# Attention feeding a mixture of experts: eight more key tiles multiplied with the values in float32

## The chip, the core and the metric

The kernel runs on 1 core of one Trainium2 chip. The metric is the device time of one execution in microseconds (us); of several executions the median is given.

## The reference

What is computed, cut to what matters (4 batches, 8 heads, 1152 keys, 576 pooled queries, head size 64):

```python
q_pool = q.reshape(B, H, S // 2, 2, D).mean(axis=3)
scores = np.matmul(q_pool, k.transpose(0, 1, 3, 2)) / np.sqrt(D)
scores = scores - np.max(scores, axis=-1, keepdims=True)
attn = np.exp(scores)
attn = attn / (np.sum(attn, axis=-1, keepdims=True) + 1e-09)
x = np.matmul(attn, v)                # all heads side by side: 2304 tokens x 512
...
h = np.maximum(x[b, s] @ w1[e], 0.0)  # e: this token's expert, by a gate on x
out[b, s] = p[e] * (h @ w2[e])
```

The change touches the product of `attn` and `v` alone.

## The kernel before, in words

The program is one order of instructions written out by hand: every engine takes its instructions in the order in which the Python code issues them, and waits where an operand isn't there. First comes the attention, then a gate that sorts tokens by expert, then the experts' two products over blocks of 128 tokens.

The attention (`attention`, L41) goes through 288 steps: 16 pairs of heads, two heads in a pair, 9 key tiles of 128 keys for each head, so 18 steps to a pair. In what follows 3:1 is step 1 of pair 3; steps 0 to 8 are the pair's first head, 9 to 17 its second. The loop at L395 issues in each step, in this order:

- `scores(s)` (L260): four TensorE matmuls of 288 columns (L268, L270) put the scores of a key tile into a PSUM tile `sc`, of which there are two, and ScalarE writes their exponentials in float32 into `ph` (L272).
- `feed_max` (L334): units of work for a later head: a matmul into a PSUM tile `psm` (L234, L240, L242; two tiles) and a VectorE maximum over it (L235, L244). The matmul that comes two units later waits for that maximum, since it needs the tile.
- preparing a later pair: GpSimd and ScalarE split keys, queries and values into two float16 parts (L155 to L203).
- in even steps `low(g)` (L278) for the two steps before. It subtracts the upper 16 bits of `ph`, read as bfloat16, from `ph` and writes the rest as float16 into `pl` (L284): a 128x576 subtraction, on GpSimd for steps 0, 2, 4, 6, 7, 10 to 14 and 16 of a pair (`LOWG`, L32), on VectorE for 1, 3, 5, 9 and 15. The other two steps, 8 and 17, have none.
- `av(s - 6)` (L296): the product of the exponentials of six steps ago with the values, added up in a PSUM tile `av`. The key tile of step 2:16 is so multiplied in step 3:4.

`av` has two forms. With float16 parts each of five query tiles takes three matmuls: upper part by the values' upper part (L310), upper by lower (L311), low part `pl` by upper (L312). In float32 (`in_f32`, L99) each query tile takes one matmul of `ph` itself by a float32 copy of the values, `vx` (L308); there `low` has nothing to do. Float32 is used for the ninth key tile of every head, and for step 13 (key tile 4 of the second head) of the nine pairs in `F32K1` (L26). `load_x` (L93) fetches the float32 values by DMA from SyncE's queue in step 8 of the pair before.

Between these steps lie smaller pieces: weights of the experts split into two parts (L586 on ScalarE, L592 on VectorE; `WSTEPS` at L463 says in which steps), the scaling of a finished head (L1302 to L1314), and for each batch of eight heads the gate's operations, one to a step, in steps of a pair that `GPL` and `GPL2` (L464, L465) allow; `GPL2` is for the third batch. Some of these use one of the two `sc` tiles under the name `wide`, as L702, L740 and L745 do, and the next `scores` but one then waits until a VectorE operation such as L741 has read it.

Of the kernel before, what the change touches and what calls it, by code (L numbers as in the profile page):

```python
# [8 lines left out]
F32 = mybir.dt.float32  # L9
# [9 lines left out]
B, H, S, D = 4, 8, 1152, 64  # L19
Q = S // 2  # L20
NKT = S // 128
# [1 line left out]
LAG = 6  # L23
LEAD = 4
SHD = 3
F32K1 = (1, 4, 5, 6, 8, 9, 12, 13, 14)  # L26
PREP0 = 13
WLEAD = 12
PRE0 = "qhb vha vl0a vl1a pqs0b pqs1b qlb loadb pkl0b pkl1b pql0b pql1b nop nop nop nop nop vhb vl0b vl1b"
# [11 lines left out]
def attention(tc, psum, stg, kT, qeo, vL, ident, emit_x, extra, load_ident, drain):  # L41
    nc = tc.nc
    V, A, G, T, SP = nc.vector, nc.scalar, nc.gpsimd, nc.tensor, nc.sync
# [5 lines left out]
    lat = late.enter_context(tc.tile_pool(name="a_late", bufs=1, side="right"))  # L49
# [6 lines left out]
    QA = [pers.tile([128, 2, Q], F16, name=f"qa{i}") for i in range(3)]  # L56

    VT = [lat.tile([128, 2, NKT - 1, 130], F16, name=f"vt{i}") for i in range(3)]
    VX = [lat.tile([128, 3, 65], F32, name=f"vx{i}") for i in range(2)]
    QD = [pers.tile([128, 128], F16, name=f"qd{i}") for i in range(3)]  # L60
    MN = [pers.tile([128, 5, 65 - 64 * i], F16, name=f"mn{i}") for i in range(2)]
    NPH = 5
    PHI = [lat.tile([128, 2 * Q + 64], F32, name=f"ph{i}") for i in range(NPH)]
# [29 lines left out]
    def load_x(p):  # L93
        b, h = divmod(2 * p, H)
        SP.dma_start(out=VX[p % 2][:, 0:2, 0:64], in_=vL[b, h:h + 2, :, 8 * D:9 * D].rearrange("h p d -> p h d"))
        if p in F32K1:
            SP.dma_start(out=VX[p % 2][:, 2, 0:64], in_=vL[b, h + 1, :, 4 * D:5 * D])

    def in_f32(n, kt):  # L99
        return kt == 8 or (kt == 4 and n % 2 == 1 and n // 2 in F32K1)  # L100

    def warm(x=None):
        x = KD[0] if x is None else x
# [171 lines left out]
    def top(x):  # L275
        return x.bitcast(BF16).rearrange("p (q two) -> p q two", two=2)[:, :, 1]

    def low(g):  # L278
        for r in range(2):
            n, kt = divmod(2 * g + r, NKT)  # L280
            if not in_f32(n, kt):
                x = G if (2 * g + r) % 18 in LOWG else V
                pf = PHI[g % NPH][:, r * Q:r * Q + Q]
                x.tensor_tensor(out=PLO[g % NPH][:, r * Q:r * Q + Q], in0=pf, in1=top(pf), op=ALU.subtract)  # L284
# [11 lines left out]
    def av(s):  # L296
        n, kt = divmod(s, NKT)
        p, j = divmod(n, 2)
        if kt == 0:
            AV[n] = ps_a.tile([128, 512], F32, name="av", tag="av")  # L300
        a = AV[n]
        ph, pl = top(PHI[s // 2 % NPH]), PLO[s // 2 % NPH]
        v = VT[p % 3]
        for t in range(5):
            o = a[:, t * 65:t * 65 + 65]
            c = (s % 2) * Q + t * 128
            if in_f32(n, kt):
                T.matmul(o, PHI[s // 2 % NPH][:, c:c + 128], VX[p % 2][:, j if kt == 8 else 2], start=False, stop=(kt == NKT - 1 and t == 4), skip_group_check=True)  # L308
                continue
            T.matmul(o, ph[:, c:c + 128], v[:, j, kt, 0:65], start=(kt == 0 and t == 0), stop=False, skip_group_check=True)  # L310
            T.matmul(o[:, 0:64], ph[:, c:c + 128], v[:, j, kt, 65:129], start=False, stop=False, skip_group_check=True)  # L311
            T.matmul(o, pl[:, c:c + 128], v[:, j, kt, 0:65], start=False, stop=(kt == NKT - 1 and t == 4), skip_group_check=True)  # L312
        if kt == NKT - 1:
            x = emit_x(n, AV.pop(n), ps_m, wide)
            later.extend(x[0])
            slow.extend(x[1])
            fast.extend(x[2])
# [46 lines left out]
    for m in MN:  # L364
        V.memset(m, 0.0)
    for x in VX:
        V.memset(x[:, :, 64:65], 1.0)
# [16 lines left out]
    f1["pkd0"]()  # L384
    f1["pkd1"]()
    load_x(0)
    f1["kl"]()
    f1["add"]()
# [6 lines left out]
    for s in range(NS + LAG):  # L395
        if s < NS:
            if not prep and nld[0] < min(NBH // 2, npr[0] + 1):
                load(nld[0])
                nld[0] += 1
            if s % 18 == 8 and s // 18 + 1 < NBH // 2:  # L400
                load_x(s // 18 + 1)
            if s % 18 == PREP0:
                p = s // 18 + 2
                if p < NBH // 2:
                    prep += prep_ops(p)
                    npr[0] += 1
            feed_shift(s)
            scores(s)
            feed_max(s)
            for _ in range(2 if s < PREP0 else 1):  # L410
                if prep:
                    prep.pop(0)()
            if s > 0 and s % 2 == 0:
                low(s // 2 - 1)
        elif s == NS:
            low(NS // 2 - 1)
        if s >= LAG:
            av(s - LAG)
# [43 lines left out]
WCD = (3, 4, 5)  # L462
WSTEPS = [30, 37, 45, 50, 54, 72, 86, 90, 125, 158, 176, 194, 230, 234, 278, 283]  # L463
GPL = {0, 1, 3, 7, 9, 13, 14, 15, 17}  # L464
GPL2 = {0, 1, 2, 5, 7, 9, 10, 11, 12, 13, 14, 15, 16, 17}  # L465
GPL1 = {9}
DMAC = {5: 0, 7: 1, 9: 0, 11: 1, 13: 0, 15: 1, 17: 0, 19: 1}
NA = 14
# [809 lines left out]
def build(tc, io, out):  # L1278
    nc = tc.nc
    V, A, G, T, SP = nc.vector, nc.scalar, nc.gpsimd, nc.tensor, nc.sync  # L1280
    with ExitStack() as ctx, tc.manual_schedule():
# [73 lines left out]
        def drain(k, wide, bank):  # L1355
# [3 lines left out]
            else:  # L1359
                first(f"d{k}")  # L1360

        tail = attention(tc, c2, m.stg, io["kT"], io["qeo"], io["vL"], m.ident2, emit_x, extra, m.load_consts, drain)
        m.open_h(c3)
        n = len(tail) - len(gate[B - 1][2])
# [28 lines left out]
```

## Time and profile before

| what | value |
|---|---|
| median of three executions | 671.71 us (670.96 to 673.86) |
| the profiled execution, its own time | 675.04 us |
| its span, from the first to the last instruction | 672.9 us |
| mean granted TensorE clock in it | 0.984 |
| TensorE matmuls busy | 642.0 us |
| VectorE busy | 552.1 us |
| ScalarE busy | 428.1 us |
| GpSimd busy | 421.4 us |
| `scores` and the products of pairs 1 to 15 | 39.80 to 417.50 us of the span |

The profile is one execution; its own time is 3.3 us over the median. A matmul's duration in it runs from its start to the end of its last column, while the next one has long begun: five matmuls of 190 ns may start 30 ns apart. So matmuls are read here by the distance between the starts of neighbours, and a step by the distance between its first `scores` matmul (L268) and the next step's. An engine's idle time says nothing by itself: what counts is the engine whose queue is never empty.

### The profile page before, as it was taken

The page shows a single profiled execution, that of the slowest core. Times are in us where ns is not written, and L with a number is a line of the kernel's source. Part 1 is how long each engine was busy: PE and PEld are TensorE (multiplying, and loading weights), DVE is VectorE, ACT ScalarE, POOL GpSimd, SP SyncE. Part 2 cuts the span into 40 slices and gives each one's busy share as a digit, 9 for nine tenths or more (in the row PEclk, how much of TensorE's full clock was granted, in tenths as well). Part 3 has the DMA queues.
Part 4 walks back from the last instruction along what each step waited for, and adds up shares of the span by engine and source line. Part 5 has one row for each costly group of instructions (what it writes and reads, how often), then busy time and mean ns, then how long its engine had stood idle before and what let it go on. Part 6 is the DMA issues. An engine that isn't in the chain of part 4 may idle for free.

```text
span 672.9 us, 22880 instructions
## 1 busy us (share of the span) xinstructions
PE 642.0 (95%) x9247; PEld 499.0 (74%) x9247; DVE 552.1 (82%) x1045; ACT 428.1 (64%) x846; POOL 421.4 (63%) x383
## 2 busy tenths in 40 slices
PE   7999999999999999999999998789999999999994
PEld 2587888888888888878887787679559649848941
DVE  7788897897998888898888897759559899899852
ACT  3678778777778677778677565559776535544500
POOL 8899999998898998898998758166000000000064
PEclk9899999999999999999999999789999999999998
DMA  8864654667474578473684307678669769777763
GB/s 245 198 173 148 201 152 111 188 163 161 140 220 113 164 180 160 139 241 90 200 181 126 108 2 133 222 236 255 208 232 325 260 237 304 287 266 260 268 235 121
DMA packets 83228, 128.80 MB, mean 191 GB/s; under 512 B 35759, under 2 KB 42031, under 8 KB 83120
## 3 DMA queue, kind: packets, MB, share of 16 engines
q1 hardware_dynamic: 79920, 117.24, 58.7%
q0 software_dynamic: 3200, 10.05, 4.3%
q8 instruction: 76, 1.25, 0.7%
q14 instruction: 32, 0.26, 0.1%
HBM read 68.82 MB, written 10.04 MB: 117 GB/s over the span
## 4 chain that ended last, share of the span: by engine, by line
PE 51%; issue 29%; DVE 10%; POOL 4%; ACT 2%; DMA 2%; another core or an unknown queue 0%; SPq 0%; POOLq 0%; DVEq 0%; ACTq 0%
PE sc L268 9%; PE sc L270 8%; PE psm L242 7%; PE av L308 6%; PE av L311 5%; PE av L310 5%; PE av L312 4%; DVE mx L244 4%; POOL out L1220 3%; DVE pl L284 2%; PE psh L257 1%; PE psh L1205 1%; PE psm L240 1%; DMA xT<-xr 1%; DVE w L592 1%
## 5 line engine op out<-in xcount | busy, mean ns | idle before, releaser
L272 ACT ACTIVATE ph<-sc 128x576 f32<-128x576 f32 x288 | 186.9, 652 | 91.8 <-PE sc L270 72.9
L244 DVE TENSOR_REDUCE mx<-psm 128x1 f32<-128x512 f32 (+1 forms) x300 | 194.1, 663 | 44.4 <-PE psm L242 41.0
L284 POOL TENSOR_TENSOR pl<-ph 128x576 f16<-128x576 f32 x167 | 207.1, 1256 | 9.0 <-ACT ph L272 9.0
L312 PE MATMUL av<-vt,pl 128*128 128x65 f16 x1235 | 138.2, 192 | 1.1 <-issue 1.1
L311 PE MATMUL av<-vt,ph 128*128 128x64 f16 x1235 | 139.1, 195 | 0.0
L310 PE MATMUL av<-vt,ph 128*128 128x65 f16 x1235 | 138.6, 193 | 0.0
L311 PEld LDWEIGHTS <-ph 128*128 128x128 bf16 x1235 | 115.3, 97 | 20.6 <-issue 0.3
L1220 POOL DMA_INDIRECT out<-acc,sid x14 | 13.7, 979 | 177.6 <-DVE acc L1129 175.4
L310 PEld LDWEIGHTS <-ph 128*128 128x128 bf16 x1235 | 116.4, 97 | 10.9 <-issue 2.9
L268 PE MATMUL sc<-qs,ks 128*128 128x288 f16 x576 | 118.0, 286 | 2.8 <-DVE st L718 1.0
L270 PE MATMUL sc<-qa,ks 65*128 65x288 f16 (+1 forms) x576 | 118.1, 286 | 0.6 <-ACT qa L258 0.6
L312 PEld LDWEIGHTS <-pl 128*128 128x128 f16 x1235 | 115.7, 99 | 1.3 <-issue 1.3
L1216 PE MATMUL pso<-w,hq 128*128 x480 | 107.4, 380 | 0.0
L592 DVE SCALAR_TENSOR_TENSOR w<-wf,w 128x512 f16<-128x512 f32 x124 | 94.3, 765 | 13.1 <-ACT w L586 12.8
L1205 PEld LDWEIGHTS <-wc 128*128 128x128 f16 x1728 | 89.2, 99 | 7.2 <-issue 6.6
L1216 PEld LDWEIGHTS <-hq 128*128 128x128 f16 (+1 forms) x576 | 45.8, 102 | 59.8 <-issue 11.7
L586 ACT ACTIVATE w<-wf 128x512 f16<-128x512 f32 x124 | 76.4, 626 | 18.0 <-DMA wf<-wq 17.8
L1205 PE MATMUL psh<-xr,wc 128*128 128x128 f16 (+1 forms) x1584 | 85.0, 212 | 1.5 <-ACT xr L1034 0.7
L242 PE MATMUL psm<-ks,qs 128*128 128x512 f16 x232 | 83.2, 379 | 0.6 <-DVE mx L244 0.6
L284 DVE TENSOR_TENSOR pl<-ph 128x576 f16<-128x576 f32 x80 | 82.4, 1030 | 1.2 <-issue 1.2
L270 PEld LDWEIGHTS <-ks 65*128 65x128 f16 (+1 forms) x576 | 56.5, 98 | 15.4 <-issue 0.8
L1071 ACT ACTIVATE hq<-psh 128x256 f16<-128x256 f32 x74 | 28.4, 384 | 52.4 <-PE psh L1205 51.6
(241 smaller groups left out, 1014.5 us busy)
## 6 DMA issues: line engine op xcount, KB each, us to landing
wf<-wq SPq DMA_DIRECT2D x124, 256.0 KB
wd<-w SPq DMA_DIRECT2D x40, 512.0 KB
ks<-kd SPq DMA_DIRECT2D x32, 288.0 KB
vf<-vL SPq DMA_DIRECT2D x16, 576.0 KB
qf<-qeo SPq DMA_DIRECT2D x15, 576.0 KB
kf<-kT SPq DMA_DIRECT2D x14, 576.0 KB
qs<-qh SPq DMA_DIRECT2D x60, 72.0 KB
ks<-kl SPq DMA_DIRECT2D x30, 144.0 KB
```

The source lines that it names most:

```text
L242: T.matmul(m[:, 0:w], q[:, t * 128:t * 128 + 128], k[:, c * 512:c * 512 + w], start=True, stop=True)
L244: V.tensor_reduce(out=mx[:, i, c:c + 1], in_=m[:, 0:w], op=ALU.max, axis=AX.X)
L268: T.matmul(sc[:, c, 0:288], ksl, QS[p][:, j, c * 288:(c + 1) * 288], start=True, stop=False)
L270: T.matmul(sc[:, c, 0:288], kal, QA[p % 3][u, j, c * 288:(c + 1) * 288], start=False, stop=True)
L272: A.activation(out=PHI[g % NPH][:, r * Q:(r + 1) * Q].rearrange("p (c q) -> p c q", c=2), in_=sc[:, :, 0:288], func=AF.Exp, scale=1.0 / 16)
L284: x.tensor_tensor(out=PLO[g % NPH][:, r * Q:r * Q + Q], in0=pf, in1=top(pf), op=ALU.subtract)
L310: T.matmul(o, ph[:, c:c + 128], v[:, j, kt, 0:65], start=(kt == 0 and t == 0), stop=False, skip_group_check=True)
L311: T.matmul(o[:, 0:64], ph[:, c:c + 128], v[:, j, kt, 65:129], start=False, stop=False, skip_group_check=True)
L312: T.matmul(o, pl[:, c:c + 128], v[:, j, kt, 0:65], start=False, stop=(kt == NKT - 1 and t == 4), skip_group_check=True)
L592: self.nc.vector.scalar_tensor_tensor(out=lo, in0=t, scalar=float(2 ** (W2S if ph % 2 else W1S)), in1=hi, op0=ALU.mult, op1=ALU.subtract)
L1205: self.nc.tensor.matmul(p[:, ft, c], u[:, ws, kk, ft * 128:ft * 128 + 128], x[:, 2 * kk + xs_, c], start=(n == 0 and ft == 0 and i == 0), ...
L1216: self.nc.tensor.matmul(p[c], h(hs, ft)[:, c], u(ws, ft), start=(first and n == 0), stop=(last and n == e), skip_group_check=(m < 128))
```

## The change

Two kinds of float32 key tiles stay as they were: the ninth of every head, and step 13 of eight of the nine pairs. A table `F32X` names further steps for each pair. Against before, 1:14, 2:16, 3:1, 3:10, 6:16, 8:1, 9:12, 12:16 and 13:15 are new, and 12:13 goes back to float16 parts: eight steps more. `vx` grows from three to five places, and `load_x` issues one DMA of 128 rows of 256 bytes for each entry. One number of `GPL2` moves, from 7 to 4.

```diff
-F32K1 = (1, 4, 5, 6, 8, 9, 12, 13, 14)
+F32X = ((), (13, 14), (16,), (1, 10), (13,), (13,), (13, 16), (), (1, 13), (12, 13), (), (), (16,), (13, 15), (13,), ())
+NVX = 3
...
-    VX = [lat.tile([128, 3, 65], F32, name=f"vx{i}") for i in range(2)]
+    VX = [lat.tile([128, 2 + NVX, 65], F32, name=f"vx{i}") for i in range(2)]
...
-        if p in F32K1:
-            SP.dma_start(out=VX[p % 2][:, 2, 0:64], in_=vL[b, h + 1, :, 4 * D:5 * D])
+        for i, x in enumerate(F32X[p]):
+            j, kt = divmod(x, NKT)
+            SP.dma_start(out=VX[p % 2][:, 2 + i, 0:64], in_=vL[b, h + j, :, kt * D:kt * D + D])
 
     def in_f32(n, kt):
-        return kt == 8 or (kt == 4 and n % 2 == 1 and n // 2 in F32K1)
+        x = n % 2 * NKT + kt
+        return n % 2 + 1 if kt == NKT - 1 else 3 + F32X[n // 2].index(x) if x in F32X[n // 2] else 0
...
-                T.matmul(o, PHI[s // 2 % NPH][:, c:c + 128], VX[p % 2][:, j if kt == 8 else 2], start=False, stop=(kt == NKT - 1 and t == 4), skip_group_check=True)
+                T.matmul(o, PHI[s // 2 % NPH][:, c:c + 128], VX[p % 2][:, in_f32(n, kt) - 1], start=False, stop=(kt == NKT - 1 and t == 4), skip_group_check=True)
...
-GPL2 = {0, 1, 2, 5, 7, 9, 10, 11, 12, 13, 14, 15, 16, 17}
+GPL2 = {0, 1, 2, 4, 5, 9, 10, 11, 12, 13, 14, 15, 16, 17}
```

Three places of the program show how it moves. In the changed kernel the lines behind the table stand one to three numbers later.

TensorE in step 3:4, the product with the key tile of 2:16 (`ph` the exponentials, `vt` the values' float16 parts, `vx` the float32 values). Before, the first of five query tiles, and the start of the next step:

```order
L234 MATMUL psm<-ks_132,qs 128x128
L310 LDWEIGHTS ph_147
L310 MATMUL av<-vt_138,ph_147 128x65
L311 LDWEIGHTS ph_147
L311 MATMUL av<-vt_138,ph_147 128x64
L312 LDWEIGHTS pl_152
L312 MATMUL av<-vt_138,pl_152 128x65
```

and now:

```order
L237 MATMUL psm<-ks_132,qs 128x128
L311 MATMUL av<-vx_139,ph_147 128x65 x5
L271 LDWEIGHTS ks_132
L271 MATMUL sc<-qs,ks_132 128x288
```

Fifteen weight loads with their matmuls became five matmuls in float32 at the same place.

VectorE from step 3:0 to step 3:6 (`mx` the maxima, `mn` their last reduction, `w` the experts' weights). Before:

```order
L592 SCALAR_TENSOR_TENSOR w_79<-wf,w_79 128x512
L244 TENSOR_REDUCE mx<-psm 128x1 x2
L284 TENSOR_TENSOR pl_153<-ph_148 128x576
L244 TENSOR_REDUCE mx<-psm 128x1
L235 TENSOR_REDUCE mx<-psm 128x4
L248 TENSOR_REDUCE mn_145<-mx 128x5
L284 TENSOR_TENSOR pl_154<-ph_149 128x576
```

and now:

```order
L595 SCALAR_TENSOR_TENSOR w_79<-wf,w_79 128x512
L247 TENSOR_REDUCE mx<-psm 128x1 x3
L238 TENSOR_REDUCE mx<-psm 128x4
L251 TENSOR_REDUCE mn_145<-mx 128x5
L287 TENSOR_TENSOR pl_154<-ph_149 128x576
```

The low part of 3:1 is gone from between two maxima; the rest of the queue moves up.

GpSimd from the end of pair 2 into pair 3 (`kl` and `ql` the lower parts of keys and queries of pair 4, `vt` its values). Before:

```order
L182 TENSOR_TENSOR kl<-kf,kd 128x576
L188 TENSOR_TENSOR ql<-qf,qh 128x576
L284 TENSOR_TENSOR pl_152<-ph_147 128x576
L203 TENSOR_TENSOR vt_137<-vf,vt_137 128x2x4x64
L284 TENSOR_TENSOR pl_153<-ph_148 128x576
```

and now:

```order
L185 TENSOR_TENSOR kl<-kf,kd 128x576
L191 TENSOR_TENSOR ql<-qf,qh 128x576
L206 TENSOR_TENSOR vt_137<-vf,vt_137 128x2x4x64
L287 TENSOR_TENSOR pl_153<-ph_148 128x576
```

The low part of 2:16 is gone from between `ql` and the values' lower part.

## Rows read from the trace of the kernel before

**Rows 1.** The page: busy time by engine (span, share), and the chain that ended last.

```profile
PE 642.0 (95%) x9247; PEld 499.0 (74%) x9247; DVE 552.1 (82%) x1045; ACT 428.1 (64%) x846; POOL 421.4 (63%) x383
...
PE 51%; issue 29%; DVE 10%; POOL 4%; ACT 2%; DMA 2%; another core or an unknown queue 0%; SPq 0%; POOLq 0%; DVEq 0%; ACTq 0%
```

**Rows 2.** Busy time by stretch: pairs 2, 3, 4, 7, 8, 10, 12, 13, 14.

```profile
core 0: us, PE busy (x) PEld busy (x) DVE busy (x) ACT busy (x) POOL busy (x), PEclk, DMA share, GB/s
66.35:90.45 24.10, 24.10 (x370) 20.24 (x367) 20.87 (x36) 19.32 (x40) 22.45 (x18) 1.00 0.56 167
90.45:114.99 24.54, 24.14 (x375) 19.63 (x372) 20.61 (x34) 18.45 (x38) 24.23 (x21) 1.00 0.50 144
114.99:139.06 24.07, 23.89 (x376) 19.64 (x372) 21.27 (x35) 18.91 (x39) 23.76 (x19) 1.00 0.60 168
...
190.17:214.41 24.24, 24.24 (x371) 20.37 (x371) 21.44 (x45) 17.57 (x36) 20.65 (x18) 1.00 0.60 181
214.41:238.23 23.82, 23.64 (x376) 19.53 (x372) 21.01 (x38) 18.50 (x38) 23.41 (x19) 1.00 0.58 159
...
264.35:290.88 26.53, 25.67 (x385) 21.14 (x382) 24.59 (x48) 20.35 (x43) 22.95 (x19) 1.00 0.50 137
...
315.00:338.83 23.83, 23.64 (x375) 19.53 (x372) 21.01 (x38) 18.51 (x39) 23.41 (x19) 1.00 0.72 174
338.83:365.23 26.40, 25.85 (x415) 21.64 (x412) 24.05 (x46) 19.71 (x42) 24.33 (x21) 1.00 0.61 162
365.23:391.93 26.70, 25.51 (x381) 21.03 (x381) 22.62 (x49) 16.82 (x35) 18.65 (x16) 1.00 0.31 95
```

**Rows 3.** Timeline of TensorE: the product in steps 1:1 (float16) and 2:1 (float32).

```profile
start us, us, engine line op out<-in xcount [idle before <-releaser]
44.02 0.19 PE L310 MATMUL av<-vt,ph 128*128 128x65 f16 x1
...
44.48 0.28 PE L268 MATMUL sc<-qs,ks 128*128 128x288 f16 x1
...
68.24 1.22 PE L308 MATMUL av<-vx,ph 128*128 128x65 f32 x10
69.30 0.29 PE L268 MATMUL sc<-qs,ks 128*128 128x288 f16 x1
```

**Rows 4.** Groups by line, shapes apart: busy us, mean ns; idle before, releaser.

```profile
L284 POOL TENSOR_TENSOR pl<-ph 128x576 f16<-128x576 f32 x167 | 207.1, 1256 | 9.0 <-ACT ph L272 9.0
...
L284 DVE TENSOR_TENSOR pl<-ph 128x576 f16<-128x576 f32 x80 | 82.4, 1030 | 1.2 <-issue 1.2
```

**Rows 5.** Timeline of pair 3, steps 3:3 to 3:7.

```profile
94.56 1.24 ACT L272 ACTIVATE ph<-sc 128x576 f32<-128x576 f32 x2
94.73 1.15 POOL L284 TENSOR_TENSOR pl<-ph 128x576 f16<-128x576 f32 x1
94.75 1.74 DVE L284 TENSOR_TENSOR pl<-ph 128x576 f16<-128x576 f32 x1
...
96.48 0.41 PE L268 MATMUL sc<-qs,ks 128*128 128x288 f16 x2
...
97.74 0.38 PE L240 MATMUL psm<-kd,qd 128*128 128x512 f16 x1 [0.22 <-DVE mx L235]
...
99.02 0.41 PE L268 MATMUL sc<-qs,ks 128*128 128x288 f16 x2
...
100.82 0.42 PE L268 MATMUL sc<-qs,ks 128*128 128x288 f16 x2
```

**Rows 6.** The same of pair 7, steps 7:5 to 7:7, where nothing waits.

```profile
196.78 0.41 PE L268 MATMUL sc<-qs,ks 128*128 128x288 f16 x2
...
198.76 0.41 PE L268 MATMUL sc<-qs,ks 128*128 128x288 f16 x2
...
200.24 0.30 PE L268 MATMUL sc<-qs,ks 128*128 128x288 f16 x1
```

**Rows 7.** The same of pair 10, step 10:5.

```profile
270.81 0.41 PE L268 MATMUL sc<-qs,ks 128*128 128x288 f16 x2
...
272.99 0.29 PE L268 MATMUL sc<-qs,ks 128*128 128x288 f16 x1
```

**Rows 8.** The same of pair 14, steps 14:3 and 14:4.

```profile
370.41 0.42 PE L268 MATMUL sc<-qs,ks 128*128 128x288 f16 x2
...
372.37 0.18 DVE L741 TENSOR_TENSOR oh<-wide,c 128x40 f16<-128x40 f32 x1
...
372.60 0.41 PE L268 MATMUL sc<-qs,ks 128*128 128x288 f16 x2 [0.85 <-DVE oh L741]
```

**Rows 9.** Waits of SyncE's queue: us in total, times, longest; then one line's DMAs.

```profile
SPq L135 <- ACT ph L272: 62.1, 10, 10.9
...
L97 SPq DMA_DIRECT2D vx<-vL x9: 457/469/1387, 27.0 to 351.1; - x9
```

**Rows 10.** Busy time in all of pairs 1 to 15: the sum over their stretches.

```profile
sum 377.70, PE 371.13 PEld 309.72 DVE 326.74 ACT 280.78 POOL 340.37; mean PE 24.74 PEld 20.65 DVE 21.78 ACT 18.72 POOL 22.69
```

## The prediction

> **What bounds the kernel now.** First the page: TensorE is busy 95% of the span and holds 51% of the chain that ended last; VectorE has 10% of it, GpSimd 4% [rows 1]. That is a mean over stages, and "busy" counts overlapping matmuls, so the next view is the busy time by pair of heads. In pairs 2 and 7 TensorE is busy for the whole stretch, 24.10 of 24.10 us and 24.24 of 24.24 [rows 2]; over pairs 1 to 15 it is idle for 377.70 - 371.13 = 6.6 us in all [rows 10]. GpSimd comes second, with 20.65 to 24.23 us busy in these stretches. The granted clock is 1.00 in all of them, the upper of the two levels (2.4 GHz), so the clock has nothing to give back here.
>
> What the reader should see in the stretches is that pairs with an extra float32 tile are not the shorter ones when nothing waits. Pair 2 holds one (1:13, multiplied in 2:1) and takes 24.10; pairs 8 and 12 hold none and take 23.82 and 23.83; pair 3 holds none and takes 24.54 [rows 2]. So there are two things to price: the float32 product itself, and the waits in pairs without it.
>
> **The float32 product.** A float16 product starts at 44.02 and the next step's scores at 44.48: 0.46 us for fifteen matmuls. A float32 one starts at 68.24 and the next scores at 69.30: 1.06 us, recorded as ten matmuls [rows 3]. Each tile that changes form costs TensorE 1.06 - 0.46 = 0.60 us. Eight more of them (nine new, one taken back) are **4.8 us** on the engine that is never empty.
>
> A page bears on this, the Trainium skill, "FP8 and Floating Point Precision", section TensorE Precision Notes: a true float32 product takes four passes through the array. With a pass as long as one float16 matmul of the trace (0.46 / 15 = 0.031 us) five query tiles would be an estimated 20 x 0.031 = 0.61 us instead of 1.06. The row differs, and I take the row; the page's case is the last rival.
>
> **What is removed.** Eight low parts: five on GpSimd (1:14, 2:16, 3:10, 6:16, 9:12; that of 12:16 goes and that of 12:13 comes back), at 1.26 us each, and three on VectorE (3:1, 8:1, 13:15), at 1.03 us [rows 4]. That is 6.3 and 3.1 us off engines with idle time. It shortens the kernel only where TensorE waits behind them.
>
> How much it waits follows from the stretches. Pair 2 without its one extra tile would take 24.10 - 0.60 = 23.50 us with no wait. Against that, pair 3 loses 24.54 - 23.50 = 1.04 us, pair 4 loses 24.07 - 23.50 = 0.57, pair 8 loses 0.32, pair 12 loses 0.33 [rows 2]. In pair 3 one sees who does it. VectorE's low part of 3:1 starts at 94.75, just behind one of GpSimd's at 94.73, and takes 1.74 us instead of 1.03; the maxima behind it are late, and the matmul of a max unit waits for L235 [rows 5]. Step 3:5 takes 99.02 - 96.48 = 2.54 us and step 3:6 takes 1.80, against 1.98 and 1.48 in pair 7 [rows 5, 6]: 0.56 + 0.32 = 0.88 of the 1.04 us. The other 0.16 stays: scores behind ScalarE's exponentials (two in a row from 94.56), which don't move.
>
> **The sum, place by place** (a tile is multiplied six steps after its scores):
>
> - 1:14, in 2:2. Pair 2 has no idle time to soak it up: **+0.60**.
> - 2:16 in 3:4 and 3:1 in 3:7. +1.20. The 0.6 us in 3:4 come just before the waits of 3:5 and 3:6, and the low part of 3:1 is gone from the queue that caused them: -0.88. **+0.32**.
> - 3:10 in 3:16. +0.60. GpSimd is one subtraction earlier when pair 4 begins, and TensorE later: most of pair 4's 0.57 should go; I take -0.45, since the same wait on ScalarE as in pair 3 (0.16) may stay. **+0.15**.
> - 6:16, in 7:4. Pair 7 is busy throughout: **+0.60**.
> - 8:1, in 8:7. Its low part is VectorE's, ahead of the max units of 8:5: -0.32. **+0.28**.
> - 9:12, in 10:0. Step 10:5 takes 272.99 - 270.81 = 2.18 us against 1.98 [rows 6, 7]; with TensorE later that 0.20 goes: **+0.40**.
> - 12:13 back to float16, 12:16 to float32: the 0.60 us move from 13:1 to 13:4; one low part for another on GpSimd. **0**, between -0.2 and +0.3, as steps 13:2 and 13:3 lose cover for up to 0.3 us of wait of the kind seen in pair 12.
> - 13:15, in 14:3. The next scores wait there: 372.60 - 370.41 = 2.19 us for a step whose work is about 1.2 (pair 7's 7:6 with its extra unit takes 1.48), because L741 on VectorE reads the `wide` tile only at 372.37 [rows 8]. L741 doesn't depend on the product, so its 0.60 us fit into that wait: **0**.
> - The number of `GPL2` moves one gate operation from 14:7 to 14:5, the gate's other operations of that lap stay; TensorE's matmuls in it are the same. **0**, 0.2 either way.
> - Eight more DMAs on SyncE, at 0.47 us each (1.39 at most) to issue, stand ahead of the key copies of L135; those wait 62 us in ten waits for ScalarE anyway [rows 9], so the cover is 6 us a time. If it failed, a pair would lose up to 1.4 us. **0**.
>
> Together 0.60 + 0.32 + 0.15 + 0.60 + 0.28 + 0.40 = **+2.35 us**. Behind the attention nothing changes; experts and gathers start that much later. The profiled execution would take 675.04 + 2.35 = 677.4; it lies 3.3 us above the median, outside the three values shown, so I add the difference to the median: 671.71 + 2.35 = **674.1 us**, 0.35% slower. A measurement of this kernel can tell about 0.5%, 3.4 us, from no change.
>
> **Bounds.** If no wait is relieved (13:15's cover aside) the cost is 4.8 - 0.6 = 4.2 us: 675.9. If all idle time of TensorE in pairs 3, 4, 8, 10, 13 and 14 is soaked up (0.40 + 0.18 + 0.18 + 0.86 + 0.55 + 1.19 = 3.36 [rows 2], and the 1.04 + 0.57 + 0.32 of waits in place of the first three's 0.76: 4.5 us), the cost is 0.3: 672.0. Values between stand nearer the forecast, since over half of that idle time (2.6 us, in pairs 10, 13 and 14) belongs to gate operations whose chain is untouched.
>
> **Rivals.**
> - *Slower: the waits stay.* What TensorE waits for in pairs 3, 4, 8 and 10 are maxima on VectorE, and a queue that is free of one low part may only wait elsewhere: VectorE also carries the weights' split at 3:0 and 4:0 and runs beside GpSimd's other subtractions, which stretch its own to 1.74 us [rows 5]. Then all that is left is the float32 product: +4.2 us, 675.9, 0.63% slower. It decides from the point where less than 1.4 of the 4.8 us is relieved. Against it: pairs 2 and 7, with GpSimd lighter ahead of them, show no wait at all [rows 2].
> - *Level: the gate's waits shrink too.* GpSimd's removed work ends contention in pairs 10, 13 and 14 as well, whose 2.6 us of idle time I left nearly untouched: the bound above, +0.3 us, 672.0. Against it: in 14:3 the wait ends with L741 on VectorE [rows 8].
> - *Faster.* For -3.4 us the change would have to relieve 8.2 us; all idle time of pairs 1 to 15 is 6.6 [rows 10], and its loss altogether would give 4.8 - 6.6 = -1.8 us, 669.9. Faster by over 0.5% needs waits that this view doesn't show, those behind back-to-back matmuls.
> - *Not float32 in earnest.* That the table is not taken up is excluded by the order of instructions: five matmuls on `vx` stand at each new step.
> - *The short float32 product.* If the new products took 0.61 us (by an estimate from rows as four passes of 0.031 us for each of five tiles), the cost would be 8 x 0.15 = 1.2 us, less the 2.4 relieved: -1.2, 670.5. The page is the Trainium skill, "FP8 and Floating Point Precision", named above; the old products of the same form took 1.06 us [rows 3], so little chance is left.
>
> **How the numbers follow.** Forecast 0.60, the waits stay 0.22, the gate's waits shrink 0.10, faster by waits not shown 0.06, short product 0.02. The forecast's own spread, about 1 us either way, puts 0.03 of it over 3.4 us, and a run's scatter (670.96 to 673.86) moves as much back from the slower rival. So faster by over 0.5% 0.06, within 0.5% 0.72, slower by over 0.5% 0.22. The range reaches from 670.8 (the level case, 672.0, less 1.2 of scatter) to 676.8 (the slower case, 675.9, plus 0.9); outside lie the faster cases and the tail of the slower one.
>
> **What would show each step.** In the changed profile: the L308 group (now L311) with 490 records at 1.06 us for ten, and 162 and 77 low parts. Pair 2 at 24.7 us and pair 7 at 24.8, both without idle time; pair 3 at 24.9, with steps 3:5 and 3:6 at about 1.98 and 1.48; pair 4 at 24.2; pair 8 at 24.1 with no wait in 8:5; pair 14 as long as before with 0.4 us of wait ahead of 14:4. The forecast is wrong if pairs 2 and 7 are not longer by 0.6, if pair 3 falls under 24.4 or stays over 25.5, or if the stretch behind the attention changes its length by over 1 us.

## The result and the profile after

Slower, by about twice what was forecast:

| | before | after | ratio, 95% interval |
|---|---|---|---|
| first session, 16 executions each | 672.28 us | 676.69 us | 1.0072 [1.0053, 1.0092] |
| second, 23 and 12 | 671.02 us | 674.12 us | 1.0050 [1.0026, 1.0075] |
| third, 19 and 10 | 671.49 us | 676.51 us | 1.0097 [1.0061, 1.0132] |

The differences of the means are 4.90, 3.74 and 5.26 us (standard errors 0.67, 0.80, 1.07); weighted by these they give **+4.6 us, 0.9 either way** (95%), against +2.35 on record. The first profiled execution took 677.66 us (span 675.5, granted clock 0.984). A line's number is 3 higher than before, so L268 is now L271, L284 is L287 and L308 is L311.

The page of the changed kernel, busy time and the chain that ended last, then two of its groups:

```profile
PE 648.1 (96%) x9207; PEld 504.4 (75%) x9207; DVE 551.0 (82%) x1042; ACT 428.9 (63%) x846; POOL 413.6 (61%) x378
...
PE 48%; issue 28%; DVE 10%; POOL 5%; DMA 4%; ACT 2%; SPq 1%; DVEq 0%; POOLq 0%; ACTq 0%
...
L287 POOL TENSOR_TENSOR pl<-ph 128x576 f16<-128x576 f32 x162 | 201.1, 1256 | 10.4 <-ACT ph L275 10.2
...
L287 DVE TENSOR_TENSOR pl<-ph 128x576 f16<-128x576 f32 x77 | 81.4, 1057 | 1.2 <-issue 1.2
```

TensorE is 6.1 us busier and GpSimd 7.8 us less than in [rows 1]; the low parts are 162 and 77 [rows 4]. What has grown in the chain is DMA, from 2% to 4%.

Busy time by stretch, changed kernel, pairs 2, 3, 4, 7, 8, 13 and 14 (columns as in [rows 2]):

```profile
69.10:93.81 24.71, 24.71 (x366) 20.94 (x363) 20.51 (x36) 19.32 (x41) 21.06 (x17) 1.00 0.57 165
93.81:119.32 25.51, 25.51 (x360) 21.62 (x357) 19.25 (x33) 19.04 (x40) 23.20 (x20) 1.00 0.48 139
119.32:142.81 23.49, 23.49 (x375) 19.54 (x372) 20.15 (x35) 18.41 (x38) 22.05 (x18) 1.00 0.61 172
194.18:219.07 24.89, 24.89 (x365) 21.02 (x365) 20.44 (x45) 17.55 (x35) 19.24 (x17) 1.00 0.59 180
219.07:243.16 24.09, 24.09 (x370) 20.23 (x367) 20.19 (x37) 18.50 (x38) 22.87 (x19) 1.00 0.58 159
...
346.23:373.51 27.28, 26.09 (x415) 21.66 (x412) 24.44 (x45) 19.63 (x43) 25.06 (x22) 1.00 0.54 148
373.51:400.12 26.61, 26.02 (x377) 21.64 (x376) 22.39 (x49) 16.78 (x35) 17.26 (x15) 1.00 0.31 94
```

TensorE now has no idle time in pairs 2, 3, 4, 7 and 8: the waits of [rows 2] are gone there, and the pairs that multiply a new tile are longer all the same; pair 4, which multiplies none, is 0.58 shorter. Most steps last the same in every trace of a kernel to about 0.02 us, so single steps can be compared between kernels. "2:2" is step 2 of pair 2, as before.

| where | forecast | measured |
|---|---|---|
| 2:2 | +0.60 | +0.60 |
| 3:4 to 3:7 | +0.32 | +0.65 - 0.55 - 0.33 + 0.60 = +0.37 |
| 3:16, pair 4 | +0.15 | +0.60 - 0.58 = +0.02 |
| 7:4 | +0.60 | +0.65 |
| 8:5, 8:7 | +0.28 | -0.34 + 0.60 = +0.26 |
| 10:0, 10:5 | +0.40 | +0.60 - 0.04 = +0.56 |
| 13:1 to 13:4 | 0 | -0.60 + 0.13 + 0.65 = +0.18 |
| 14:3 | 0 | 0 |
| `GPL2` in pairs 14 and 15 | 0 | +0.15 - 0.24 + 0.20 = +0.11 |
| sum in the attention | **+2.35** | **+2.75** |
| 5:14, a DMA's wait | 0 | +0.44 on average |
| behind the attention | 0 | +1 to +2 |

The last two lines are what the forecast lacked; where they come from took the experiments. The relief of the waits is seen in TensorE's timeline of the changed kernel, steps 3:4 to 3:7:

```profile
98.66 0.40 PE L271 MATMUL sc<-qs,ks 128*128 128x288 f16 x2
...
100.49 0.41 PE L271 MATMUL sc<-qs,ks 128*128 128x288 f16 x2
...
102.48 0.41 PE L271 MATMUL sc<-qs,ks 128*128 128x288 f16 x2
...
103.95 0.42 PE L271 MATMUL sc<-qs,ks 128*128 128x288 f16 x2
```

Step 3:5 takes 1.99 us and 3:6 1.47, against 2.54 and 1.80 in [rows 5] and 1.98 and 1.48 in [rows 6].

### The profile page after: what moved, and what is told of

It reads as the page before. It is cut to its first block, busy times and chain, and to the rows that moved or that the text cites. A ratio compares the mean times of both kernels' runs of the same rounds, so it can differ in the third digit from the quotient of the medians.

```text
span 675.5 us, 22792 instructions
## 1 busy us (share of the span) xinstructions
PE 648.1 (96%) x9207; PEld 504.4 (75%) x9207; DVE 551.0 (82%) x1042; ACT 428.9 (63%) x846; POOL 413.6 (61%) x378
## 4 chain that ended last, share of the span: by engine, by line
PE 48%; issue 28%; DVE 10%; POOL 5%; DMA 4%; ACT 2%; SPq 1%; DVEq 0%; POOLq 0%; ACTq 0%
PE sc L271 9%; PE sc L273 8%; PE av L311 6%; PE psm L245 6%; PE av L314 4%; PE av L313 4%; PE av L315 4%; DVE mx L247 3%; POOL out L1223 3%; DMA gkf<-xs,gid 2%; DVE pl L287 2%; PE psh L260 1%; POOL pl L287 1%; PE psm L243 1%; DMA xT<-xr 1%
## 5 line engine op out<-in xcount | busy, mean ns | idle before, releaser
L287 POOL TENSOR_TENSOR pl<-ph 128x576 f16<-128x576 f32 x162 | 201.1, 1256 | 10.4 <-ACT ph L275 10.2
L314 PE MATMUL av<-vt,ph 128*128 128x64 f16 x1195 | 134.6, 195 | 0.0
L315 PE MATMUL av<-vt,pl 128*128 128x65 f16 x1195 | 133.7, 192 | 0.7 <-DVE pl L287 0.7
L313 PE MATMUL av<-vt,ph 128*128 128x65 f16 x1195 | 134.1, 193 | 0.0
L314 PEld LDWEIGHTS <-ph 128*128 128x128 bf16 x1195 | 111.5, 97 | 20.1 <-issue 0.3
L313 PEld LDWEIGHTS <-ph 128*128 128x128 bf16 x1195 | 112.6, 97 | 12.0 <-issue 4.2
L271 PE MATMUL sc<-qs,ks 128*128 128x288 f16 x576 | 118.6, 288 | 1.8 <-DVE st L721 1.0
L315 PEld LDWEIGHTS <-pl 128*128 128x128 f16 x1195 | 112.0, 99 | 0.8 <-DVE pl L287 0.8
L595 DVE SCALAR_TENSOR_TENSOR w<-wf,w 128x512 f16<-128x512 f32 x124 | 92.1, 747 | 13.0 <-ACT w L589 12.7
L287 DVE TENSOR_TENSOR pl<-ph 128x576 f16<-128x576 f32 x77 | 81.4, 1057 | 1.2 <-issue 1.2
L311 PEld LDWEIGHTS av<-vx,ph 128*128 128x128 f32 x490 | 61.8, 191 | 5.2 <-issue 2.0
```

Of the source, the lines that this page charges most:

```text
L271: T.matmul(sc[:, c, 0:288], ksl, QS[p][:, j, c * 288:(c + 1) * 288], start=True, stop=False)
L311: T.matmul(o, PHI[s // 2 % NPH][:, c:c + 128], VX[p % 2][:, in_f32(n, kt) - 1], start=False, stop=(kt == NKT - 1 and t == 4), skip_group_c ...
```

## Experiments

### The parts of the change

The number of `GPL2` alone, in the kernel before:

```
-GPL2 = {0, 1, 2, 5, 7, 9, 10, 11, 12, 13, 14, 15, 16, 17}
+GPL2 = {0, 1, 2, 4, 5, 9, 10, 11, 12, 13, 14, 15, 16, 17}
```

> The kernel before with the one number of GPL2 moved and nothing else. Place by place (each tile costs 0.60 us less the waits it covers, +2.4 us in all, as forecast): 0, between -0.3 and +0.3 us. Full price (each of eight tiles costs 0.60 us, nothing comes back, +4.8 us): 0. Moved gate work (what the forecast lacked, some 2.4 us, comes from gate operations that now meet GpSimd's subtractions): +1 to +2.5 us.

Ratio 0.9988 [0.9949, 1.0028]. In the attention 14:5 +0.15, 14:7 -0.24, 15:9 +0.19. By this run's time `GPL2` costs nothing, though the interval reaches to +1.9 us; the traces and the second run of it (gpl2_b, below) say otherwise.

The tiles alone, the old `GPL2`:

> The change without the number of GPL2. Place by place: +2.4 us, and what the whole change adds to that would have to come from GPL2. Full price: +4.8 us. Moved gate work: about +2.4 us, if GPL2 is what moves it; +4 to +5 us if the longer products alone shift the gate's operations against GpSimd's.

Ratio 1.0065 [1.0031, 1.0099], every place of the table up to 14:3 as in the change but 10:0, which is +0.97 in this trace.

The low parts of the nine new tiles computed although nobody reads them (`if not in_f32(n, kt)` gets `or ... in KEEP`):

> The change, but the nine low parts are still computed on GpSimd and VectorE, though nothing reads them: TensorE's work is the changed kernel's, the other engines' that of before. Place by place: the waits that only the later TensorE covers (0.56 in step 3:5, 0.2 in 10:5, 0.6 in 14:3) still go, those that went with the low parts (0.32 in 3:6, 0.45 in pair 4, 0.32 in 8:5) stay, so about 1.1 us over the changed kernel. Full price: the same as the changed kernel, +4.8 us, since the low parts are worth nothing.

Ratio 1.0120 [1.0056, 1.0184]. In the trace 3:6 keeps most of its wait (+0.23 against the change), 8:5 keeps its own (+0.33), and 4:5, where TensorE waits for maxima, gets 0.65 more than before. The two waits that go although the low parts are computed are 3:5, where the new tile in 3:4 gives cover, and 4:6, for which 4:5 pays. So the relief in 3:6, pair 4 and 8:5 needs the low parts gone; TensorE's being later is not enough.

No extra tile at all (`F32X` empty, old `GPL2`):

> The other way: the changed kernel's code with an empty table and the old GPL2, so that all nine extra float32 tiles of before become float16 too. Full price: 9 x 0.60 = 5.4 us faster than before. Place by place: -5.4, and each pair behind one gets the waits of the pairs without: 0.33 (as pairs 8 and 12) to 1.04 (as pair 3), nine of them, 3 to 6 us with two at the upper end: between -2.4 and +0.5 us.

Ratio 1.0040 [1.0005, 1.0075]. The nine old tiles of step 13 go, -0.60 each, but waits for maxima come in the steps behind (5:5 +0.51, 5:6 +0.33; 10:5 +0.64, 10:6 +0.61). Pairs 2, 5, 6, 7, 10 and 15 are longer by 0.14 to 0.66 us without their tile: those tiles return more than they cost.

### A wait that comes and goes

The first trace of the change held 2.87 us more in 11:15, 11:17, 12:0 and 12:5, where nothing was changed: small gate operations on VectorE that took 1.2 to 1.3 us each. Two kernels were aimed at it. First, pair 9's tile left out, `(12, 13)` to `(13,)`:

> The change without its tile 9:12, which goes back to float16 parts. The traces of the changed kernel and of the change without GPL2 both lose 2.9 us in steps 11:15 to 12:5, behind small gate operations of VectorE that take 1.2 to 1.9 us there instead of 0.2 to 0.7; the four other traces don't. Race that the change sets up (GpSimd's queue, one subtraction shorter from 9:12 on, meets the gate's operations otherwise): without 9:12 the 2.9 us are gone too, so 3.4 us less than the changed kernel, +1 to +1.8 us over before. Chance (the same waits come and go from execution to execution in any kernel): 0.6 us less than the changed kernel. Full price (0.60 us a tile, nothing comes back): 0.6 less, +4.2 over before.

Ratio 1.0051 [1.0024, 1.0079]; the wait is there. Then one gate operation a step later, `(f, gp - {13} if b == 1 and f is o7c else gp)`:

> The changed kernel with one gate operation of the second batch (the rank's two integer operations, L764 and L765, of pair 11) one step later, and those behind it moved up by as much; no other instruction changes. Race that the change sets up: the 2.9 us in 11:15 to 12:5 go, or shrink to under 1 us; +1.5 to +2.5 us over before. Chance and full price: the same as the changed kernel, +4.4 to +4.8.

Ratio 1.0178 [1.0147, 1.0208], worse: 12:0 +2.40, 12:5 +0.46, and in this trace a stretch at the lower clock inside the attention (granted 0.50, 1.2 GHz, from 354.9 to 361.7 us; 13:7 to 13:9 +5.95). A miss; why all six of its executions take 680 us and more is not shown. The changed kernel and the kernel before, once more:

> The changed kernel again, for a second trace and a second measurement beside the two above. Race that the change sets up: steps 11:15 to 12:5 lose 2.9 us again. Chance: they may not. Time: +4.4 to +4.8 us over before by either.

> The kernel before again, one look. What is the same in both traces of it belongs to the program, what differs to the execution: the start (pair 0), the wait for the transposed tokens in 9:14 (1.0 us in the first trace) and step 13:15 (1.1 us longer in four of the five other traces) should differ; pairs 1 to 8, 11 and 12 should agree within 0.05 us, and 11:15 to 12:5 show no loss. Chance: 11:15 to 12:5 may lose time here too.

Neither trace has the wait, so its presence in the change's first trace proved little; a count was needed.

> The changed kernel again, to count how often the wait in steps 11:15 to 12:5 comes. Theory A (the wait is set up by the change: three of four traces with the change's tiles had it, none of five without it or with the low parts kept): the four steps 11:15, 11:17, 12:0 and 12:5 are together 2.5 to 3.0 us longer than in the trace of before, with chance 0.75. Theory B (it is an accident that comes to either kernel alike, 3 in 9): chance 0.33. Both: the changed tiles' own steps stand as in the earlier traces of the change to 0.05 us (2:2 +0.60, 7:4 +0.65, 10:0 +0.60, 13:1 -0.60 and 13:4 +0.65), the ratio is 1.004 to 1.008.

> The kernel before, again. Theory A: no wait in 11:15 to 12:5, each of the four steps within 0.1 us of the first trace. Theory B: it is there with chance 0.33.

That settled it: after_l3 lacks it, and this trace of the kernel *before* has it, to the hundredth (+0.23, +0.63, +1.56, +0.46). VectorE and GpSimd in two traces of the kernel before, first without the wait (before_again), then with it (before_l3):

```profile
309.83 0.16 DVE L762 TENSOR_SCALAR ji<-vi 128x5 int32<-128x5 int32 x1
309.85 2.24 POOL L284 TENSOR_TENSOR pl<-ph 128x576 f16<-128x576 f32 x2
310.94 0.16 DVE L768 CAST jl<-ji 128x5 f32<-128x5 int32 x1
```

```profile
308.75 1.19 DVE L762 TENSOR_SCALAR ji<-vi 128x5 int32<-128x5 int32 x1
308.77 2.25 POOL L284 TENSOR_TENSOR pl<-ph 128x576 f16<-128x576 f32 x2
310.96 1.33 DVE L768 CAST jl<-ji 128x5 f32<-128x5 int32 x1
```

The same instruction starts 0.02 us ahead of the same subtraction both times; once it takes 0.16 us, once as long as a subtraction. Over all 17 traces in which this part of the gate is untouched the wait came in 2 of 8 with the old tiles or none and in 3 of 9 with the new ones. So it doesn't take the change to bring it, and these counts don't show that the change makes it likelier. Two other waits come and go with the old tiles and with the new, one of 1.4 us in 13:15 to 14:0 and one of up to 1.7 us in 9:14.

One kernel more had been aimed at it, with one small VectorE operation a step (the two casts on ScalarE: `A.activation(out=rf, in_=ri, func=AF.Copy)`, the shift one step later), in two traces:

> The changed kernel; of the second batch's gate the shift on VectorE goes from the step of the mask (11:15) to the step behind it (11:17), and the two casts go from VectorE to ScalarE, so that VectorE has one small gate operation to a step from 11:15 to 12:0 where it had two in 11:15 and in 11:17. Theory A (VectorE gets one instruction in between two of GpSimd's subtractions, and the second small one loses by about 20 ns and waits for a whole subtraction): the wait of 2.9 us is gone or under 0.6 us in this trace and in the second one, 11:15 and 11:17 within 0.15 us of before; the ratio falls to 1.002 to 1.005. Rival C (the wait is of the subtraction pl itself or of the one-hot operation L776, whatever stands ahead of it): 12:0 and 12:5 keep +1.5 to +2.0 us in at least one of the two traces, ratio 1.004 to 1.008.

> The same kernel as the one ahead of it, a second trace. Theory A: again no wait of over 0.6 us in 11:15 to 12:5; if chance alone had taken it away, two traces without it would come with 0.25 times 0.25, about 0.06. Rival C: 12:0 and 12:5 together over +1.5 us in one of the two.

Ratio 1.0052 [1.0025, 1.0079]. Neither theory: 11:15 to 12:0 are as before in both traces, but 12:5 and 12:6 get +0.90 and +0.62 in both, behind the next small operation (L783, 1.18 us). The wait has moved to a later operation; that it is the same conflict there is not shown.

### The stretch behind the attention, and SyncE's queue

> The nine tiles without the new GPL2, a second look at what lies behind the attention. In the traces so far, from the last scores to the end, executions with little low clock there take 253.2 us in the kernel before (two of them) and 254.7 to 256.3 us in the changed one (four). Theory D (the new GPL2 delays the first gather behind the attention): here the time behind the last scores is that of before, 253.2 us within 0.5 us plus half of the additional low-clock time, GpSimd's last subtraction of L1317 starts 5.79 us ahead of the last scores, and the ratio is lower than the changed kernel's, 1.003 to 1.006. Theory E (the tiles do it, by the phase in which TensorE and the DMAs meet): 254.7 to 256.3 us here too, ratio 1.006 to 1.008. Attention as in the first trace of this kernel, less the waits that come and go.

> The kernel before with the new GPL2 alone, a second look at the same place. Theory D: 254.7 to 256.3 us behind the last scores, GpSimd's last subtraction of L1314 5.55 us ahead of them, ratio 1.001 to 1.004. Theory E: 253.2 us within 0.5 us plus half of the additional low-clock time, ratio 0.998 to 1.001.

Ratios 1.0048 [1.0023, 1.0074] and 1.0041 [1.0003, 1.0079]. Two theories were on record: D, that the new number of `GPL2` delays the first gather of tokens behind the attention, and E, that the tiles do. The traces tell them apart. "The last scores" are the first `scores` matmul of step 15:17. In each of the four fences that follow: GpSimd's issue of the first gather of tokens, the last float32 product of the attention, TensorE's first transposition of gathered tokens, the experts' first product. The kernel before (before_l3), its number ahead of all:

```profile
416.55 1.14 POOL L1019 DMA_INDIRECT gkf<-xs,gid  x1 [0.17 <-issue]
...
418.59 1.31 PE L308 MATMUL av<-vx,ph 128*128 128x65 f32 x10
421.83 0.62 PE L1031 MATMUL av<-ident,gkf 128*128 128x128 f16 x8 [1.21 <-DMA gkf<-xs,gid]
424.88 1.33 PE L1205 MATMUL av<-xr,wc 128*128 128x128 f16 x11 [0.29 <-ACT xr L1034]
```

The nine tiles with the old `GPL2` (tiles_b; of the float32 product nine of ten records are there, so it may have begun 0.11 us earlier):

```profile
417.56 1.13 POOL L1022 DMA_INDIRECT gkf<-xs,gid  x1 [0.17 <-issue]
...
419.77 1.17 PE L311 MATMUL av<-vx,ph 128*128 128x65 f32 x9
422.90 0.62 PE L1034 MATMUL av<-ident,gkf 128*128 128x128 f16 x8 [1.23 <-DMA gkf<-xs,gid]
425.88 1.44 PE L1208 MATMUL av<-xr,wc 128*128 128x128 f16 x12 [0.35 <-ACT xr L1037]
```

The kernel before with the new `GPL2` (gpl2_b), its L1314 and L1019 on GpSimd too:

```profile
405.91 0.83 POOL L1314 TENSOR_TENSOR xr<-xf,xr 128x320 f16<-128x320 f32 x1 [2.27 <-ACT xr L1311]
406.70 7.25 POOL L284 TENSOR_TENSOR pl<-ph 128x576 f16<-128x576 f32 x6
414.12 1.45 POOL L1019 DMA_INDIRECT gkf<-xs,gid  x1 [0.18 <-issue]
...
415.59 1.30 PE L308 MATMUL av<-vx,ph 128*128 128x65 f32 x10
420.26 1.04 PE L1031 MATMUL av<-ident,gkf 128*128 128x128 f16 x8 [2.24 <-DMA gkf<-xs,gid]
423.94 1.44 PE L1205 MATMUL av<-xr,wc 128*128 128x128 f16 x12 [0.29 <-ACT xr L1034]
```

The changed kernel, first trace:

```profile
422.93 1.76 POOL L1022 DMA_INDIRECT gkf<-xs,gid  x1 [0.17 <-issue]
...
424.40 1.30 PE L311 MATMUL av<-vx,ph 128*128 128x65 f32 x10
428.81 1.04 PE L1034 MATMUL av<-ident,gkf 128*128 128x128 f16 x8 [2.38 <-DMA gkf<-xs,gid]
432.49 1.44 PE L1208 MATMUL av<-xr,wc 128*128 128x128 f16 x12 [0.29 <-ACT xr L1037]
```

From the last product to the experts' first it is 6.29 and 6.11 us with the old number, 8.35 and 8.09 with the new one. Of that 0.35 us is the last product's starting earlier; from the last scores it is 10.76 and 10.75 us against 12.48 and 12.23. The wait for the first gather is 1.2 us with the old, 2.2 to 2.4 with the new. What the number of `GPL2` does there stands in VectorE's order (`-` the kernel before, `+` gpl2_b): it moves not only the gate operation of 14:7 but also the selection L829 of pair 15, ahead of the head's scaling L1302 and a low part.

```
-L1302 TENSOR_SCALAR rc<-av 128x5
 L829 TENSOR_TENSOR wf<-oh,wf 128x120
 L830 TENSOR_REDUCE wf<-wf 128x15
-L284 TENSOR_TENSOR pl_153<-ph_148 128x576
-L1305 RECIPROCAL rc<-rc 128x5
+L1302 TENSOR_SCALAR rc<-av 128x5
 L829 TENSOR_TENSOR wf<-oh,wf 128x120
 L830 TENSOR_REDUCE wf<-wf 128x15
+L284 TENSOR_TENSOR pl_153<-ph_148 128x576
+L1305 RECIPROCAL rc<-rc 128x5
```

The scaling ends later, GpSimd's L1314 waits 2.27 us for ScalarE's part of it instead of 1.30, and the six low parts and the gather queued behind it are 0.24 us late against the last scores. The gather's issue takes 1.45 to 1.78 us instead of 1.14, and from its start to the transposition it is 5.9 to 6.9 us in all eleven traces with the new number, 4.9 to 5.8 in seven with the old (7.3 and 9.1 in the two others); why it lands later is not shown. TensorE's clock falls to 1.2 GHz in this stretch in every trace, for 6.8 us in six of the nine with the old number and for 10.2 in eight of the eleven with the new; whether the later gather brings that is not shown either.

Theory D holds, by trace. From the last scores to the end, in traces with at most 16 us at the lower clock behind the attention, it is 253.2 to 255.5 us with the old number (six traces, mean 254.2) and 254.7 to 256.3 with the new one (seven, mean 255.6): 1 to 2 us. The line at 16 us was drawn afterwards. Of the traces it leaves out, three with the old number and three with the new take 259.6 to 265.0 us, for a reason not shown, and a fourth with the new takes 255.9; over all twenty the medians are 255.0 and 256.2, the means 256.9 and 257.7. By times alone the number's share is not measured: 0.9988 and 1.0041 for it alone.

> The kernel before with nothing in float32 added; the low parts of steps 3:1, 4:1 and 8:1 go from VectorE to GpSimd. If VectorE's low part is what makes 3:5, 3:6 and 8:5 wait, the waits go without the 0.60 us that a float32 tile costs: 3:5 and 3:6 together 0.6 to 0.9 us shorter, 8:5 0.3 us, pair 4 0 to 0.5 us shorter, pairs 1 to 15 in all 0.9 to 1.7 us shorter than before's, ratio 0.997 to 1.000 (less than a measurement can tell, so the steps decide). Rival: GpSimd, 1.15 us later behind 3:1, delivers its own low parts or the key parts too late and a wait comes in the same pairs or the next: pairs 3, 4 and 8 within 0.3 us of before or longer.

In the kernel before, three low parts go from VectorE to GpSimd (`in LOWG or 2 * g + r in LOWX`, with `LOWX = (55, 73, 145)`). Ratio 1.0034 [1.0004, 1.0064], the rival. 3:5 -0.56, 4:6 -0.34 and 8:5 -0.33 go as forecast, 3:6 keeps its wait against the forecast (+0.05), and 3:8 +0.94, 4:8 +0.89 and 8:8 +0.65 come. TensorE and GpSimd of this kernel in 3:8 (lines 1 higher than before):

```profile
100.87 4.45 POOL L285 TENSOR_TENSOR pl<-ph 128x576 f16<-128x576 f32 x4
...
100.37 0.41 PE L269 MATMUL sc<-qs,ks 128*128 128x288 f16 x2
102.06 0.20 PE L313 MATMUL av<-vt,pl 128*128 128x65 f16 x1 [0.76 <-POOL pl L285]
102.47 0.41 PE L269 MATMUL sc<-qs,ks 128*128 128x288 f16 x2
```

VectorE's low part was the cause of the waits in 3:5, 4:6 and 8:5, and GpSimd has no room for it. What holds 3:6 is not settled: it is relieved in the changed kernel alone, where the low part is gone and the tile in 3:4 gives cover.

> The kernel before, a further trace, to count what comes and goes: the wait of 2.9 us in 11:15 to 12:5 (so far in one of three traces of before, in one of three of the changed kernel), the wait of 1.4 us in 13:15 to 14:0 (two of three, one of three) and the low clock at the start (one of three, three of three). Each should come with a chance between a third and two thirds if it is an accident that comes to either kernel alike. Behind the last scores 253.2 us plus half of any additional low-clock time.

No wait in 11:15 to 12:5 and none in 13:15; low clock at the start, and 255.5 us behind the last scores with 15.3 us of it at the lower clock, where before_l3 has 8.9 and takes 253.2. In 9:14 to 9:16 it holds 2.8 us more than before_l3, with 3.4 us there at the lower clock: that too comes without the change.

The other place is 5:14. It was 0.24 to 0.99 us longer in nine of the ten traces with the added DMA of pair 6, unchanged in the tenth and, to 0.1 us, in the eight without. SyncE's queue and TensorE in after_l3, then SyncE's queue in before_l3:

```profile
153.95 0.83 SPq L96 DMA_DIRECT2D vx<-vL  x1
154.83 1.35 SPq L99 DMA_DIRECT2D vx<-vL  x2
156.22 2.73 SPq L626 DMA_TRANSPOSE xT<-xr  x1
...
162.55 1.06 PE L664 MATMUL wide<-wgh,xT 128*128 128x18 f16 x36 [0.47 <-DMA xT<-xr]
```

```profile
150.62 0.52 SPq L95 DMA_DIRECT2D vx<-vL  x1
151.18 0.65 SPq L97 DMA_DIRECT2D vx<-vL  x1
151.88 2.95 SPq L623 DMA_TRANSPOSE xT<-xr  x1
```

The fetches of `vx` stand just ahead of the last transposition of the gate's tokens, and TensorE waits for that in 5:14. Taking them behind it (`s % 18 == (13 if s // 18 == 5 else 8)`), with the new and with the old `GPL2`:

> The changed kernel with the float32 values of pair 6 fetched in step 5:13 in place of 5:8, so that neither they nor the added DMA stand ahead of the transposition of the gate's tokens in SyncE's queue. In nine of ten traces with the added DMA step 5:14 is 0.24 to 0.99 us longer than before's (0.44 on average over all ten), in none of eight without it. If the DMA's place in the queue is the cause, 5:14 is within 0.1 us of before here (or shorter) and all else stands as in the change: ratio 1.004 to 1.008. Rival: the wait comes from the tiles' later arithmetic or from traffic, and 5:14 stays 0.2 us or more longer.

> The same with the old GPL2: what is left are the nine tiles alone, whose steps came to +2.6 us. 5:14 again within 0.1 us of before; the first product of the experts 10.8 us behind the last scores when the clock there is low for under 3 us; ratio 1.002 to 1.006, lower than the changed kernel's. If the ratio is the changed kernel's, 1.005 to 1.008, the two places (5:14 and the stretch behind the attention) are not what separates forecast and measurement.

5:14 is +0.15 and +0.12 in place of +0.44, just over the 0.1 forecast, and the trace shows no DMA wait there any more: by one trace of each, most of it was the queue, and a little stays. In late_oldgpl2 the first expert product is 10.64 us behind the last scores, as before. Its pairs 1 to 15 are as the table says, but the ratios are 1.0140 [1.0100, 1.0180] (5 executions) and 1.0082 [1.0045, 1.0119] (8), higher than forecast and as wide as what they should resolve. The first says that the fetch moved out of the way made the kernel slower, if anything. Times don't confirm here what the steps show.

## Why the prediction was wrong

Right: the price of a tile, 0.60 us (0.65 in 3:4, 7:4 and 13:4); that pairs 2 and 7 have no cover; the relief in 3:5 and 3:6 and its size; the relief in pair 4 and 8:5 by the low parts that went; the free tile of 13:15 in 14:3; no float32 product shorter than 1.06 us. The slower rival, "the waits stay", comes near the measured time (+4.2) for the wrong reason: the waits went.

Small misses in the attention, +0.40 together: the 0.20 us of 10:5 stayed (-0.04), the exchange of 12:13 for 12:16 cost 0.18, `GPL2` 0.11; pair 4 gave 0.13 more than taken. Pair 3 was told as 24.9 us and pair 4 as 24.2, although 3:16 lies in pair 3; they are 25.5 and 23.5.

What failed is two terms put at zero.

- "The number of `GPL2` moves one gate operation from 14:7 to 14:5 ... **0**, 0.2 either way" and "Behind the attention nothing changes". It moves an operation of pair 15 too, on VectorE, ahead of the scaling that GpSimd waits for, and behind GpSimd's last low parts stands the first gather, for which TensorE then waits: 1 to 2 us in the traces. The prediction had named this stretch's changing by over 1 us as a sign of its being wrong.
- "Eight more DMAs on SyncE ... stand ahead of the key copies of L135 ... If it failed, a pair would lose up to 1.4 us. **0**." I asked what the key copies wait for; the transpositions of the gate's tokens stand in the same queue, and there pair 5 lost 0.44 us on average.

2.75 + 0.44 + (1 to 2) = 4.2 to 5.2 us, against 4.6 measured, 0.9 either way. Of the kernels that take the sum apart, the times agree for the nine tiles with the old `GPL2`: 3.1 us by their steps, 4.4 and 3.2 by the ratios of tiles_only and tiles_b. With the late fetch they do not: with the old `GPL2` it should cost 2.8 us and measured 3.0 to 8.0, with the new one 3.9 to 4.9 and measured 6.7 to 12.1. So the two terms are shown by steps in traces and not by times, and executions that weren't profiled may hold more; that stays open. Whether the lower clock at the start (in 2 of 8 traces without the new tiles, in 7 of 12 with them; pair 0 takes 26.0 and 27.1 us on average) has to do with the change is open as well. Against it stands the mean granted clock of whole executions, which hardly differs: 0.986 before and after in the second session, 0.987 in the third.

## What to carry to other kernels

A table of allowed steps moves every operation of its lap, not the one you looked for: list all the places where the order differs, and follow the last one to what stands behind it in the queue of a second engine. An added DMA is priced against the tightest consumer in its queue, not the one with the longest wait. Before a wait in one trace is put down to a change, count it in several traces of both kernels.

## What the hardware showed

A small VectorE operation that starts 0.02 us ahead of a GpSimd subtraction takes 0.16 us or 1.19 us, from one execution of the same program to the next. The Trainium skill, "SBUF — State Buffer", section Who interferes with whom, says that the two engines share one pair of ports as an exclusive lock and that the loser waits for the whole instruction. The 1.19 us agree, as one subtraction takes 1.14 us here; that a record which starts first can lose is what the rows add.

The lower clock at the start came without a difference in what TensorE had done. Stretches of the nine tiles with the old `GPL2` (tiles_only), then of the kernel without pair 9's tile (no912):

```profile
12.00:16.00 4.00, 3.67 (x20) 1.41 (x20) 3.97 (x8) 0.39 (x1) 3.14 (x3) 1.00 1.04 304
16.00:20.00 4.00, 3.39 (x16) 1.09 (x15) 2.62 (x5) 3.41 (x8) 0.53 (x1) 0.89 1.05 234
20.00:24.00 4.00, 4.00 (x18) 1.82 (x16) 3.65 (x6) 2.29 (x4) 4.00 (x4) 0.50 0.78 138
```

```profile
12.00:16.00 4.00, 3.67 (x20) 1.41 (x20) 3.97 (x8) 0.40 (x1) 3.15 (x3) 1.00 1.05 309
16.00:20.00 4.00, 3.39 (x16) 1.08 (x16) 2.81 (x6) 3.42 (x8) 0.53 (x1) 1.00 1.04 235
20.00:24.00 4.00, 2.97 (x26) 1.94 (x26) 3.87 (x6) 3.20 (x6) 4.00 (x4) 1.00 0.79 137
```

Up to 19.1 us TensorE's matmuls start at the same times, to 0.02 us. There the clock of the one falls (0.89 granted over the second stretch, 0.50 in the third, 1.2 GHz), and the other keeps 1.00 (2.4 GHz); pair 0 took 29.1 and 25.5 us.
